# Later maxima for batch 1, another order of weight tiles, and casts on VectorE in an attention + FFN kernel

## The chip, the core and the metric

One NeuronCore of a Trainium2 chip runs the whole program. The metric is the device time of one execution in microseconds; the median of 3 runs before is 716.87 us (716.13 to 718.10). In this text PE is TensorE, DVE is VectorE, ACT is ScalarE, SP is the engine whose queue issues the loads and stores.

## The reference

Linear-memory attention in 8 batches of 8 heads, 576 tokens, head size 64, 32 memory slots, and a SiLU feed-forward layer over all tokens:

```python
a = exp(phi - max(phi, axis=2)); a = a / (sum(a, axis=2) + 1e-9)      # [8, 8, 576, 32]
k_m = einsum('bhsm,bhsd->bhmd', a, k); v_m = einsum('bhsm,bhsd->bhmd', a, v)
scores = q @ k_m.T / sqrt(64)
attn = softmax(scores); x = (attn @ v_m) as [4608, 512]
h = x @ w_in            # w_in [512, 2048]
g = h * sigmoid(h)
out = g @ w_out         # w_out [2048, 512], all float32
```

## The kernel before, in words

Inputs are float32 in a layout made beforehand; the two weights come as 64-bit words, which the kernel itself turns into float32. To keep float32 accuracy, every large product is done as three products of a high part and a low part: `wo_hi`/`wo_lo` for w_out, `ghi`/`glo` (both in the tile `gparts`) for the activations, `ahi`/`alo` (`aparts`) for the attention and two halves of `pparts` for the product of v_m and w_in, which replaces x @ w_in: first p = v_m @ w_in per head, then h = attn @ p.

**The main loop.** For each batch b there are 16 steps, one for each 128 columns of d_ff. Step fc does `ffn1` on PE (12 matmuls into the one PSUM tile `h`), `silu` on ACT (`g`, 512 tokens, and `gleft`, 64 tokens; `h` is free when gleft is done), `split` (ghi is a cast of g, glo is g minus ghi), and then, in two halves of two token tiles each, `ffn2` of the step before: per token tile three matmuls, ghi by wo_hi, ghi by wo_lo, glo by wo_hi, into `acc`. After every second batch four `left` steps do the remaining tokens.

**Slots.** All other work hangs on a table `events`: `ev(b, slot, fn)` puts fn behind a half step; slot 5 is behind the first half of step 5's ffn2, slot 5.5 behind its second half. In batch 0 these are the p tiles (`p_mm`, 256 columns each, at 2.5, 4.5, 6.5 ...), the conversions of the weights (`conv_next`) and the attention of batch 1, whose slots stand in `at_slot`: mx (maxima of phi, `phi_max` on DVE), sub (the maxima brought together by transposes on PE, `phi_allmax`, and half a step later back to all partitions, and `phi_sub`), ex (`phi_exp` on ACT), em (`e_mm`: 80 matmuls into `bg`, then `kvn`, k_m and v_m normalised, one half by ACT, one by DVE), tr (`e_tr`: kvn transposed on PE, copied to `kvT`), s0 and s1 (scores), and the softmax. `bg` is one PSUM tile: p tiles, maxima, e, transposes and scores all use it in turn, and each waits until the one before has been read out (for a p tile by `p_split`: hi on ACT, lo on DVE, line 575).

**Weights.** Both are cut in 8 tiles of 256 columns or rows, here called i0 to i7 (w_in) and o0 to o7 (w_out). `w_load` brings a tile into `raw`, of which there are 3 buffers; a tile of w_in comes in two halves. Two early tiles, o1 and i2, have a home inside `win` instead. `w_conv` turns a tile into float32: two ACT instructions (lines 166 and 168), a shift and an add on DVE (lines 170 and 172), and for w_out two more, wo_hi on ACT (174) and wo_lo on DVE (176). Then its raw buffer is free. `conv_next` converts the next tile of the list `to_conv` and then asks for the next of `to_load`. Tile i(j) is needed by the p tile at slot 2j-1.5, tile o(j) by ffn2 in step 2j+1.

**What sets the order.** PE and SP keep the order in which the program is written; in batch 0 the order of DVE and ACT is chosen by the framework's scheduler when the program is built and then is fixed. Each engine takes its instructions in that order and waits at the head. So a load that waits for a raw buffer holds up every load behind it on SP.

Of the kernel before, what the change touches and what calls it, by code (L numbers as in the profile page):

```python
# [24 lines left out]
DMODEL, DFF = 512, 2048  # L25
NFC = DFF // P
CW = 256
# [21 lines left out]
def attn_ffn_kernel(  # L49
# [9 lines left out]
    nc = tc.nc  # L59
# [115 lines left out]
            elif kind == "o":  # L175
                nc.vector.tensor_tensor(wo_lo[:, fc], to, wo_hi[:, fc], op=ALU.subtract)  # L176

    to_load = iter([(k, j) for j in range(1, DFF // CW) for k in "io"])
    to_conv = iter([(k, j) for j in range(1, DFF // CW) for k in "io"])

    def load_next(few=False):
        w = next(to_load, None)
# [396 lines left out]
    def ffn1(b, fc):  # L579
        hi, lo = pj[b, fc * P // JW]  # L580
        fs = slice(fc * P % JW, fc * P % JW + P)
        ahi, alo = at[b]["ahi"], at[b]["alo"]
        h = ps.tile([P, 2, 512], F32, tag="h", name="h", bufs=1)
        for hf in range(2):
            sl = slice(hf * HALF, (hf + 1) * HALF)
            n = 0
            for wt, a in ((hi, ahi), (hi, alo), (lo, ahi)):
                for p in range(2):
                    nc.tensor.matmul(h[:, hf, :HALF], wt[:, p, fs], a[:, p, sl], start=n == 0, stop=n == 5)  # L589
                    n += 1  # L590
        return h

    turn = iter(range(1 << 30))

    def split(g32, on_act=False, steps=(0, 1), gs=None):
        if gs is None:
            n = next(turn) % 2
            gs = gparts[:, 0, n], gparts[:, 1, n]
        ghi, glo = gs
        if 0 in steps:  # L600
            if on_act:
                nc.scalar.copy(ghi, g32)  # L602
            else:
                nc.vector.tensor_copy(ghi, g32)  # L604
        if 1 in steps:
            nc.vector.tensor_tensor(glo, g32, ghi, op=ALU.subtract)  # L606
        return gs

    def silu(b, fc, h):
        g32 = sb.tile([P, MAIN], F32, tag="g32", name="g32", bufs=2)  # L610
        w = MAIN // 2
        nc.scalar.activation(g32.rearrange("p (h f) -> p h f", h=2), h[:, :, :w], AF.Silu)  # L612
        o = b % 2 * LEFT
        nc.scalar.activation(  # L614
            gleft[:, fc, o : o + LEFT].rearrange("p (h f) -> p h f", h=2), h[:, :, w:HALF], AF.Silu
        )
        return g32
# [36 lines left out]
    def ev(b, slot, fn, *a):  # L654
        events.setdefault((b, slot), []).append((fn, a))

    for b in range(B):
        if b == 0:
            for j in range(2, DFF // CW):
                ev(b, 2 * j - 1.5, p_mm, b, j * CW, CW)  # L660
        else:
            for j in range(1, NJ):
                ev(b, 4 * j - 3, p_mm, b, j * JW, JW)
        n = b + 1
        if n == B:
            continue
        at_slot = (2, 3, 4, 5.5, 7.5, 9.5, 11.5, 11.5, 12, 12.5, 12.5, 13) if b == 0 else (0, 1, 2, 3, 4, 6, 7, 8, 9, 10, 11, 12)
        mx, sub, ex, em, tr, s0, s1, sx, se, ss, sn, sk = at_slot
        ev(b, mx, phi_max, n)
        if n == 1:  # L670
            ev(b, sub, phi_allmax, n, (0, 1), (0,))
            ev(b, sub + 0.5, phi_allmax, n, (0, 1), (1,))
        else:
            for i in range(3):
                ev(b, sub, phi_fold, n, i)
        ev(b, sub + 0.5, phi_sub, n)
        ev(b, ex, phi_exp, n)
        ev(b, em, e_mm, n)
        if n + 1 < B:
            ev(b, 14 if b == 0 else em + 1, load_kv, n + 1)  # L680
        ev(b, tr, e_tr, n)
        ev(b, s0, s_mm, n, 0)
        ev(b, em, load_q, n, 1)
        ev(b, s1, s_mm, n, 1)
        if n + 1 < B:
            ev(b, s1, load_q, n + 1, 0)
        ev(b, sx, s_max, n, ALL)
        ev(b, sx, s_sub, n, ALL)
        ev(b, se, s_exp, n, ALL)
        ev(b, ss, s_sum, n, ALL)  # L690
        ev(b, sn, s_norm, n, ALL)
        ev(b, sk, s_back, n, ALL)
        ev(b, sk, s_low, n, ALL)
        if n + 1 < B:
            ev(b, sk, load_phi, n + 1)
        ev(b, 14, p_mm, n, 0, JW)
    for k in range(1, DFF // CW * 2 - 2):
        ev(0, max(1.5, k - 1), conv_next)

# [8 lines left out]
    with in_order(DVE, ACT) as last:  # L710
# [62 lines left out]
        w_conv(O0, 0, "hal")  # L773
        w_conv(I1, None, "p")
        gs = split(silu(0, 0, ffn1(0, 0)))
        w_conv(I1, None, "csa")
        w_conv(O0, 1, "sh")
        g32 = silu(0, 1, ffn1(0, 1))
        g1 = split(g32, steps=(0,))
        main_step(0, 0, gs, (0, 1))  # L780
        p_mm(0, CW, CW)
        main_step(0, 0, gs, (2, 3))
        split(g32, steps=(1,), gs=g1)
        w_conv(O0, 1, "al")
        prev = ("main", 0, 1, g1)
# [8 lines left out]
    def finish(tiles):  # L794
        if prev is None:
            return
        if prev[0] == "main":
            main_step(prev[1], prev[2], prev[3], tiles)
        elif tiles[0] == 0:
            left_step(prev[1], prev[2], prev[3])  # L800

    for b in range(B):
        if b == 1:
            whole.close()
        for fc in range(NFC):
            if b == 0 and fc < 2:
                for part in range(2):
                    for fn, a in events.pop((b, fc + part / 2), []):
                        fn(*a)
                continue  # L810
            h = ffn1(b, fc)
            gs = split(silu(b, fc, h), b == 0 and fc < 7)
            for part in range(2):
                finish((2 * part, 2 * part + 1))
                for fn, a in events.pop((b, fc + part / 2), []):
                    fn(*a)
            prev = ("main", b, fc, gs)
        if b % 2:
            for n in range(NLS):
                gs = split(gleft[:, n * NI : (n + 1) * NI].rearrange("p c f -> p (c f)"))  # L820
                finish((0, 1, 2, 3))
                prev = ("left", b, n, gs)
# [3 lines left out]
def build(arrays, bacc, num_devices=1):  # L826
    nc = bacc.Bacc("TRN2", target_bir_lowering=False, num_devices=1, dynamic_dma_scratch_size=1024)
    aps = [
        nc.dram_tensor(n, a.shape, mybir.dt.from_np(a.dtype), kind="ExternalInput").ap() for n, a in arrays.items()
    ]  # L830
    out = nc.dram_tensor("out", (B * S, DMODEL), F32, kind="ExternalOutput").ap()
    with tile.TileContext(nc) as tc:
        attn_ffn_kernel(tc, *aps, out)
    return nc
# [44 lines left out]
```

## Time and profile before

| what | before |
|---|---|
| median of 3 runs | 716.87 us |
| the profiled execution | 715.9 us, its span 714.1 us |
| PE busy | 696.7 us, 98% of the span |
| DVE busy, ACT busy | 364.6 us (51%), 260.7 us (37%) |
| granted PE clock | 0.999 |

The span runs from the first to the last instruction of the program. Rows of the order of time read: start, length, engine, line, operation, tiles, and in brackets the idle time of the engine just before and the instruction that ended it. Rows of a group read: busy us, mean ns of one, then idle us before them. Busy PE is not PE at its peak. Line numbers are those of the kernel before; in the changed one they differ by one or two.

### The profile page before, as it was taken

To read this page: it belongs to the slowest core of one execution; us is meant where nothing else is said; L and a number is where in the kernel's file an instruction comes from. 1 tells how busy PE (TensorE), PEld (TensorE's weight loads), DVE (VectorE), ACT (ScalarE), POOL (GpSimd) and SP (SyncE) were. 2 spreads that over 40 slices of the span, in tenths; PEclk is the share of its full clock that TensorE was granted. 3 is DMA by queue.
4 is the path that set the end of the run, shared out by engine and by line. 5 is a ranking of instruction groups with operands and counts; after the bars stand their busy time and mean duration, and the time that the engine had idled before them with its cause. 6 is when DMAs were issued, how large, how long until landed. Compare 5 with 4: busy or idle time off the path is not lost.

```text
span 714.1 us, 11570 instructions
## 1 busy us (share of the span) xinstructions
PE 696.7 (98%) x4833; PEld 556.4 (78%) x4833; DVE 364.6 (51%) x653; ACT 260.7 (37%) x459; POOL 0.7 (0%) x6
## 2 busy tenths in 40 slices
PE   7879999999999999999999999999999999999997
PEld 3567677878888788877888778787888878888885
DVE  3897877356353563637346373635636355233322
ACT  2799744324223242524124241332322324132211
POOL 0000000000000000000000000000000000000000
PEclk9999999999999999999999999999999999999999
DMA  9967605321023210132010320131101000010002
GB/s 344 388 232 241 238 34 226 134 68 34 1 74 133 68 34 1 60 139 74 23 60 15 135 71 30 61 134 67 34 9 65 2 1 1 0 60 1 1 1 74
DMA packets 25444, 60.14 MB, mean 84 GB/s; under 512 B 2096, under 2 KB 10416, under 8 KB 25392
## 3 DMA queue, kind: packets, MB, share of 16 engines
q1 hardware_dynamic: 24672, 57.02, 22.8%
q10 hardware_dynamic: 720, 2.38, 0.9%
q8 instruction: 38, 0.62, 0.4%
q14 instruction: 14, 0.11, 0.1%
HBM read 49.95 MB, written 9.44 MB: 83 GB/s over the span
## 4 chain that ended last, share of the span: by engine, by line
PE 82%; DVE 5%; ACT 5%; issue 1%; DMA 1%; DVEq 0%; ACTq 0%; SPq 0%
PE acc L626 44%; PE h L589 25%; PE accleft L626 6%; PE bg L559 4%; PE bg L309 2%; PE bg L353 1%; DMA raw<-in_w_in 1%; DVE gparts L606 1%; ACT L612 1%; ACT g L612 1%; ACT phi L297 1%; DVE wo_lo L176 1%; ACT pparts L573 1%; DVE phi L289 1%; ACT raw L168 1%
## 5 line engine op out<-in xcount | busy, mean ns | idle before, releaser
L626 PE MATMUL acc<-wo_hi,gparts 128*128 128x512 f32 x1024 | 352.1, 397 | 0.5 <-DVE gparts L606 0.5
L626 PEld LDWEIGHTS acc<-wo_hi,gparts 128*128 128x128 f32 x1024 | 192.0, 188 | 66.8 <-issue 29.8
L589 PEld LDWEIGHTS h<-aparts,pparts 128*128 128x128 f32 x1536 | 215.2, 188 | 17.9 <-ACT gleft L614 5.6
L589 PE MATMUL h<-aparts,pparts 128*128 128x288 f32 x1536 | 225.9, 296 | 1.8 <-ACT gleft L614 1.1
L626 PE MATMUL acc<-wo_lo,gparts 128*128 128x512 f32 x512 | 201.2, 393 | 0.4 <-DVE wo_lo L176 0.4
L612 ACT ACTIVATE g<-h 128x512 f32<-128x512 f32 x128 | 76.4, 597 | 305.4 <-issue 179.6
L604 DVE CAST gparts<-g 128x512 fp32r<-128x512 f32 x123 | 52.3, 425 | 220.7 <-ACT g L612 219.9
L626 PEld LDWEIGHTS acc<-wo_lo,gparts 128*128 128x128 f32 x512 | 96.1, 188 | 15.2 <-DVE wo_lo L176 0.7
L606 DVE TENSOR_TENSOR gparts<-g,gparts 128x512 fp32r<-128x512 f32 x128 | 88.1, 688 | 11.9 <-ACT gparts L602 1.3
L575 DVE TENSOR_TENSOR pparts<-bg,pparts 128x1024 fp32r<-128x1024 f32 (+1 forms) x36 | 39.5, 1098 | 37.4 <-ACT pparts L573 37.4
L573 ACT ACTIVATE pparts<-bg 128x1024 fp32r<-128x1024 f32 (+1 forms) x36 | 33.3, 926 | 28.8 <-PE bg L559 28.8
L626 PE MATMUL accleft<-wo_hi,gparts 128*128 128x512 f32 x128 | 40.6, 389 | 0.0
L559 PE MATMUL bg<-win,kvT 64*32 64x512 f32 (+1 forms) x576 | 35.8, 554 | 0.9 <-DVE win L172 0.8
L614 ACT ACTIVATE gleft<-h 128x64 f32<-128x64 f32 x128 | 28.0, 219 | 0.0
L626 PEld LDWEIGHTS accleft<-wo_hi,gparts 128*128 128x128 f32 x128 | 24.0, 188 | 4.9
L632 ACT ACTIVATE o<-acc 128x512 f32<-128x512 f32 x32 | 19.1, 598 | 21.3 <-PE acc L626 10.7
L626 PE MATMUL accleft<-wo_lo,gparts 128*128 128x512 f32 x64 | 24.9, 389 | 0.0
L612 ACT ACT_TABLE_LOAD x14 | 18.0, 1283 | 8.0 <-PE h L589 7.9
L559 PEld LDWEIGHTS bg<-win,kvT 64*32 64x32 f32 x576 | 6.6, 104 | 14.3 <-issue 12.9
L604 DVE CAST gparts<-gleft 128x512 fp32r<-128x512 f32 x16 | 6.8, 427 | 20.7 <-PE accleft L626 12.2
L168 ACT ACTIVATE raw<-raw 128x1024 int32<-128x1024 uint32 (+1 forms) x16 | 16.5, 1030 | 0.0
L391 DVE TENSOR_REDUCE ssm<-sc 128x36 f32<-128x1152 f32 x7 | 9.5, 1353 | 8.8 <-ACT sc L387 8.8
(123 smaller groups left out, 369.3 us busy)
## 6 DMA issues: line engine op xcount, KB each, us to landing
kv<-in_kv SPq DMA_DIRECT2D x28, 516.0 KB, 6.2
q<-in_q SPq DMA_DIRECT2D x16, 576.0 KB, 3.8
out<-o SPq DMA_DIRECT2D x32, 256.0 KB, 2.1
raw<-in_w_in SPq DMA_DIRECT2D x14, 512.0 KB, 6.6
raw<-in_w_out SPq DMA_DIRECT2D x6, 1024.0 KB, 6.4
phi<-in_phi SPq DMA_DIRECT2D x7, 576.0 KB, 3.8
kv<-in_kv ACTq DMA_DIRECT2D x4, 516.0 KB, 6.2
kr<-in_kv SPq DMA_DIRECT2D x7, 258.0 KB, 7.4
```

What stands on the lines that cost most here:

```text
L168: nc.scalar.activation(r, low, AF.Copy, scale=2.0**-29)
L309: nc.tensor.matmul(pt[p][M * r : M * (r + 1), :KVW], e[:, p, c, M * r : M * (r + 1)], kvt[c][:, p, r], start=c == 0, stop=False, skip_grou ...
L559: nc.tensor.matmul(bg[M * r : M * (r + 1), p, :w].rearrange("p (k f) -> p k f", f=P), kvT[D * p : D * (p + 1), 1, r], win[D * p : D * (p + ...
L573: nc.scalar.activation(hi[:, :, c], bg[:, :, :w], AF.Copy)
L575: nc.vector.tensor_tensor(lo[:, :, c], bg[:, :, :w], hi[:, :, c], op=ALU.subtract)
L589: nc.tensor.matmul(h[:, hf, :HALF], wt[:, p, fs], a[:, p, sl], start=n == 0, stop=n == 5)
L604: nc.vector.tensor_copy(ghi, g32)
L606: nc.vector.tensor_tensor(glo, g32, ghi, op=ALU.subtract)
L612: nc.scalar.activation(g32.rearrange("p (h f) -> p h f", h=2), h[:, :, :w], AF.Silu)
L614: nc.scalar.activation(gleft[:, fc, o : o + LEFT].rearrange("p (h f) -> p h f", h=2), h[:, :, w:HALF], AF.Silu)
L626: nc.tensor.matmul(acc[key], gt[:, cs], wt[:, fc], start=fc == 0 and n == 0, stop=fc == NFC - 1 and n == 2)
L632: nc.scalar.activation(o, acc.pop(key), AF.Copy)
```

## The change

Three edits.

1. The first four attention slots of batch 1 in batch 0 move: mx 2 to 4, sub 3 to 5, ex 4 to 6, em 5.5 to 7.5; tr moves from 7.5 to 8. The slots from s0 on stay.
2. Tiles are asked for and converted in another order: i(j+1) ahead of o(j). Conversions were i2 after o1, then o2, i3, o3, i4 ... at slots 2, 3, 4, 5 ...; now i2 comes ahead of o1, and then i3 at 3, o2 at 3.5, i4 at 5, o3 at 5.5, i5 at 7, o4 at 7.5, up to o7 at 12.5.
3. ghi of steps 2 to 6 of batch 0 was cast by ACT; now DVE casts all.

```diff
-    to_load = iter([(k, j) for j in range(1, DFF // CW) for k in "io"])
-    to_conv = iter([(k, j) for j in range(1, DFF // CW) for k in "io"])
+    later = [w for j in range(2, DFF // CW) for w in (("i", j + 1), ("o", j))][:-2] + [("o", DFF // CW - 1)]
+    to_load = iter([("i", 1), ("o", 1), ("i", 2)] + later)
+    to_conv = iter([("i", 1), ("i", 2), ("o", 1)] + later)
...
-    def split(g32, on_act=False, steps=(0, 1), gs=None):
+    def split(g32, steps=(0, 1), gs=None):
...
-            if on_act:
-                nc.scalar.copy(ghi, g32)
-            else:
-                nc.vector.tensor_copy(ghi, g32)
+            nc.vector.tensor_copy(ghi, g32)
...
-        at_slot = (2, 3, 4, 5.5, 7.5, 9.5, 11.5, 11.5, 12, 12.5, 12.5, 13) if b == 0 else (0, 1, 2, 3, 4, 6, 7, 8, 9, 10, 11, 12)
+        at_slot = (4, 5, 6, 7.5, 8, 9.5, 11.5, 11.5, 12, 12.5, 12.5, 13) if b == 0 else (0, 1, 2, 3, 4, 6, 7, 8, 9, 10, 11, 12)
...
-    for k in range(1, DFF // CW * 2 - 2):
-        ev(0, max(1.5, k - 1), conv_next)
+    for slot in [1.5, 1.5] + [2 * j - 1 if k == "i" else min(2 * j - 0.5, 12.5) for k, i in later for j in [i - 1 if k == "i" else i]]:
+        ev(0, slot, conv_next)
...
-            gs = split(silu(b, fc, h), b == 0 and fc < 7)
+            gs = split(silu(b, fc, h))
```

How the order of the engines moves, at three places. First SP, the loads behind the first half of batch 1's q (in a row of `in_w_in` two halves of one tile). Before: o2, i3, o3, i4, o4, i5.

```order
L87 DMA q1_0_428<-in_q 128x1152
L87 DMA raw_430<-in_w_out 128x2x512
L87 DMA raw_432<-in_w_in 128x4x128 x2
L87 DMA raw_435<-in_w_out 128x2x512
L87 DMA raw_444<-in_w_in 128x4x128 x2
L87 DMA raw_451<-in_w_out 128x2x512
L87 DMA raw_490<-in_w_in 128x4x128 x2
```

Now: i3, o2, i4, o3, i5, o4, i6.

```order
L87 DMA q1_0_428<-in_q 128x1152
L87 DMA raw_430<-in_w_in 128x4x128 x2
L87 DMA raw_433<-in_w_out 128x2x512
L87 DMA raw_435<-in_w_in 128x4x128 x2
L87 DMA raw_442<-in_w_out 128x2x512
L87 DMA raw_451<-in_w_in 128x4x128 x2
L87 DMA raw_523<-in_w_out 128x2x512
L87 DMA raw_538<-in_w_in 128x4x128 x2
```

With three buffers taken in turn, i5 now takes the buffer of o2; before, the tile in the fourth place, i4, took it.

Second DVE, from the conversion of i2 and o1 to the maxima of batch 1 (`mt`, `mx`); g_466 here is g of step 2, g_523 of step 3. Before, with no cast, since ACT did it:

```order
L172 ISA win<-win,cva 128x1024x2
L172 ISA win<-win 128x2048
L176 TENSOR_TENSOR wo_lo<-win,wo_hi 128x1024
L606 TENSOR_TENSOR gparts<-g_466,gparts 128x512
L238 TENSOR_TENSOR mt<-phi_416 128x512
L170 TENSOR_SCALAR cva<-cva 128x1024
L239 TENSOR_TENSOR mx<-mt 128x256
L172 ISA raw<-raw,cva 128x1024x2
L241 TENSOR_TENSOR mx<-mx,phi_416 64x128 x2
L176 TENSOR_TENSOR wo_lo<-raw,wo_hi 128x1024
L575 TENSOR_TENSOR pparts<-bg,pparts 128x2x256
L606 TENSOR_TENSOR gparts<-g_523,gparts 128x512
```

Now the same stretch holds no maxima; g_467 is g of step 2, g_508 of step 3.

```order
L172 ISA win<-win 128x2048
L172 ISA win<-win,cva 128x1024x2
L602 CAST gparts<-g_467 128x512
L176 TENSOR_TENSOR wo_lo<-win,wo_hi 128x1024
L604 TENSOR_TENSOR gparts<-g_467,gparts 128x512
L576 TENSOR_TENSOR pparts<-bg,pparts 128x2x256
L602 CAST gparts<-g_508 128x512
L170 TENSOR_SCALAR win<-win 128x1024
L604 TENSOR_TENSOR gparts<-g_508,gparts 128x512
L172 ISA win<-raw,win 128x2048
L170 TENSOR_SCALAR cva<-cva 128x1024
L172 ISA raw<-raw,cva 128x1024x2
```

i2's add (`win<-win`) now stands ahead of o1's, pparts ahead of o2, and the maxima follow behind o2's add.

Third ACT, ahead of its half of kvn (g_621 is g of step 5, g_699 of step 7, g_795 of step 8). Before, kvn stood between steps 5 and 6:

```order
L612 ACTIVATE g_621<-h 128x512
L614 ACTIVATE gleft<-h 128x64
L602 CAST gparts<-g_621 128x512
L166 ACTIVATE cva<-raw 128x1024
L168 ACTIVATE raw<-raw 128x1024
L174 ACTIVATE wo_hi<-cva 128x1024
L166 ACTIVATE win<-raw 128x1024
L168 ACTIVATE raw<-raw 128x1024
L331 ACTIVATE kvn<-bg,rs 128x2x64
```

Now, between steps 7 and 8:

```order
L610 ACTIVATE g_699<-h 128x512
L612 ACTIVATE gleft<-h 128x64
L168 ACTIVATE raw<-raw 128x1024
L174 ACTIVATE wo_hi<-cva 128x1024
L166 ACTIVATE win<-raw 128x1024
L168 ACTIVATE raw<-raw 128x1024
L166 ACTIVATE cva<-raw 128x1024
L168 ACTIVATE raw<-raw 128x1024
L332 ACTIVATE kvn<-bg,rs 128x2x64
L610 ACTIVATE g_795<-h 128x512
```

Five conversion instructions stood between g and kvn before, six now, of the tiles o4, i6 and o5, and the cast is gone.

## The prediction

> **What bounds the kernel now.** I read the page first, then who waited for whom on PE, then PE's order of time between 36 and 112 us, then the same stretch on DVE, ACT and the load queue, with groups of lines for the prices.
>
> ```profile
> span 714.1 us, 11570 instructions
> ...
> PE 696.7 (98%) x4833; PEld 556.4 (78%) x4833; DVE 364.6 (51%) x653; ACT 260.7 (37%) x459; POOL 0.7 (0%) x6
> ```
>
> PE sets the end: only its idle time can be won or lost. Between step 2 of batch 0 and the scores of batch 1 it stands five times, 0.36+0.78+2.85+0.48+1.15 = 5.62 us together; that is all the change can reach. In order of time (start, length, engine, line, operation; idle time before and what ended it in brackets):
>
> ```profile
> 39.07 0.50 PE L626 MATMUL acc<-wo_lo,gparts 128*128 128x512 f32 x1 [0.36 <-DVE wo_lo L176]
> ...
> 42.64 0.67 PE L559 MATMUL bg<-win,kvT 64*32 64x256 f32 x16 [0.78 <-DVE win L172]
> 43.23 1.86 PE L589 MATMUL h<-aparts,pparts 128*128 128x288 f32 x12
> ...
> 49.33 0.44 PE L250 MATMUL bg<-ident,mx 128*128 128x128 f32 x2 [2.85 <-DVE pparts L575]
> ...
> 51.36 1.83 PE L589 MATMUL h<-aparts,pparts 128*128 128x288 f32 x12
> ...
> 56.46 1.85 PE L589 MATMUL h<-aparts,pparts 128*128 128x288 f32 x12
> ...
> 63.27 1.86 PE L589 MATMUL h<-aparts,pparts 128*128 128x288 f32 x12
> ...
> 72.99 0.38 PE L339 MATMUL bg<-ident,kvn 128*128 128x128 f32 x2
> ...
> 81.34 0.73 PE L626 MATMUL acc<-wo_hi,gparts 128*128 128x512 f32 x2 [0.48 <-DVE gparts L606]
> ...
> 85.06 0.72 PE L353 MATMUL bg<-q,kvT 64*32 64x288 f32 x16 [1.15 <-DVE pparts L575]
> ...
> 101.25 1.85 PE L589 MATMUL h<-aparts,pparts 128*128 128x288 f32 x12
> ...
> 105.69 1.75 PE L589 MATMUL h<-aparts,pparts 128*128 128x288 f32 x12
> ```
>
> Step lengths follow: a bare step 105.69-101.25 = 4.44; with a p tile 56.46-51.36 = 5.10; with e's 80 matmuls 63.27-56.46 = 6.81. Why PE waits there is on DVE and ACT, nearly full from 36 to 92 us:
>
> ```profile
> 36.00:92.00 56.00, 50.20 (x412) 38.98 (x411) 48.64 (x71) 49.56 (x67) 0.00 (x0) 1.00 0.65 224
> ```
>
> (Columns: PE, PEld, DVE 48.64 of 56, ACT 49.56 of 56.) The grant stays at 1.00, so the clock takes no part.
>
> **The 2.85 us** is DVE's backlog: the maxima, o1's and o2's conversions and the release of bg by `p_split` queue up:
>
> ```profile
> 39.54 0.69 DVE L170 TENSOR_SCALAR win<-win 128x1024 uint32<-128x1024 uint32 x1
> ...
> 41.27 1.22 DVE L172 CUSTOM_DVE_ANT_0 win<-win 128x2048 uint16<-128x2048 uint16 x1
> 42.41 1.23 DVE L176 TENSOR_TENSOR wo_lo<-win,wo_hi 128x1024 fp32r<-128x1024 f32 x1
> ...
> 44.16 0.67 DVE L238 TENSOR_TENSOR mt<-phi 128x512 f32<-128x512 f32 x1
> ...
> 45.71 1.21 DVE L172 CUSTOM_DVE_ANT_0 raw<-raw,cva 128x2048 uint16<-128x2048 uint16 x1
> ...
> 47.45 1.23 DVE L176 TENSOR_TENSOR wo_lo<-raw,wo_hi 128x1024 fp32r<-128x1024 f32 x1
> 48.59 0.68 DVE L575 TENSOR_TENSOR pparts<-bg,pparts 128x512 fp32r<-128x512 f32 x1
> ```
>
> Back to back, a row of 1.22 starts the next 1.14 later (47.45 to 48.59), one of 0.69 0.60 later. With that I walk the new DVE order. From 38.9: two shifts 1.20, two adds 2.28, the cast of step 2 0.34, wo_lo of o1 1.14, glo 0.61, pparts 0.60: 45.1. The cast of step 3 waits for ACT's g until 45.2, then cast 0.34, shift 0.60, glo 0.61, i3's add 1.14, shift 0.60, o2's add 1.14, i4's shift 0.60, mt 0.60, wo_lo of o2 1.22: it ends at **52.2**. Then cast, mx, glo, two small mx and pparts, which ends about 54.5 and frees bg. The maxima's transposes stand ahead of step 5's third tile, where PE comes at 52.1+1.7+1.4 = 55.2 (below): 2.85 goes to 0. Their second half, behind DVE's cm, is ready at 56.5 and wanted at 56.8; I leave 0.1 for both.
>
> **The 0.78 us** goes: i2's adds now stand ahead of o1's, one 1.22 us row earlier, where 0.78 was missing. The price is o1: ghi's cast and glo of step 2 now have `wo_lo` of o1 between them (cast at 42.4, wo_lo at 42.8, glo 43.9 to 44.6), and PE wants glo at about 44.4: 0.3 lost.
>
> **The 1.15 us** belongs to i7, which was late:
>
> ```profile
> 73.76 0.93 SPq L87 DMA_DIRECT2D raw<-in_w_in  x2
> ...
> 82.55 1.13 ACT L166 ACTIVATE win<-raw 128x1024 f32<-128x1024 f32 x1 [3.13 <-DMA raw<-in_w_in]
> ```
>
> ACT stood 3.13 us before it with the eviction of bg behind it. In the new order i7 is asked for when o4's buffer is free, about 71, so it lands about 76 and this wait goes. The 0.48 (glo behind o6's adds) goes too; the 0.36 lies ahead of the change and stays.
>
> **The casts.** Five go from ACT to DVE:
>
> ```profile
> L602 ACT CAST gparts<-g 128x512 fp32r<-128x512 f32 x5 | 3.1, 619 | 0.0
> ...
> L604 DVE CAST gparts<-g 128x512 fp32r<-128x512 f32 x5 | 2.1, 418 | 1.2 <-ACT g L612 1.2
> ...
> L606 DVE TENSOR_TENSOR gparts<-g,gparts 128x512 fp32r<-128x512 f32 x10 | 6.8, 683 | 1.4 <-ACT gparts L602 1.3
> ```
>
> ACT gains 3.1 - 5x0.1 of overlap = 2.6 us, DVE loses 5x0.34 = 1.7. DVE has 7.4 us idle in the stretch, ACT 6.4, so neither sum decides; bounds are a gain of 1.3 (the wait L606 had for ACT) and a loss of 1.7 if every cast lay on the path. I take 0: both are already inside the walk along the new order that gives the other terms.
>
> **What costs nothing.** The exp moves with its two table loads, as many as before, and they are in ACT's sum below. q's second half moves with e's slot behind o6 on the load queue, asked for at about 73; even at i7's 8.3 it lands by 82, and the second scores of step 11 want it about 91. Without that cover it would cost what i7 cost, 1.15.
>
> **What is late next: e.** The order before gave e's matmuls and the transposes of kvn two steps: 72.99-63.27 = 9.7 us on PE. Now they are half a step apart: ffn1 and two tiles, 1.7+1.4 = 3.1 us. When does PE arrive, when is kvn ready?
>
> PE: step 3 starts at 42.2; + 4.44+0.3 = 47.0 (step 4); + 5.10 = 52.1; + 4.44 and 0.55 for the maxima's small matmuls = 57.1; + 5.10 = 62.2; + 6.81 = 69.0 (step 8); + 3.1 = 72.1.
>
> kvn: it hangs on i5. i5's buffer is o2's and comes free when DVE has written wo_lo of o2, at 52.2 by the walk above. What a tile of w_in takes from there, and what ACT's rows cost:
>
> ```profile
> 57.26 0.92 SPq L87 DMA_DIRECT2D raw<-in_w_in  x2
> ...
> DMA to landing us min/median/max: 3.7/4.2/4.8
> ...
> L168 ACT ACTIVATE raw<-raw 128x1024 int32<-128x1024 uint32 x11 | 12.6, 1144 | 0.0
> L174 ACT ACTIVATE wo_hi<-cva 128x1024 fp32r<-128x1024 f32 x7 | 7.4, 1059 | 0.3 <-DVE cva L170 0.3
> L166 ACT ACTIVATE cva<-raw 128x1024 f32<-128x1024 f32 x6 | 7.1, 1177 | 0.7 <-DVE kvT L342 0.7
> L166 ACT ACTIVATE win<-raw 128x1024 f32<-128x1024 f32 x5 | 5.8, 1153 | 3.1 <-DMA raw<-in_w_in 3.1
> ...
> L612 ACT ACT_TABLE_LOAD x1 | 1.3, 1283 | 0.0
> ...
> 56.88 1.17 ACT L297 ACTIVATE phi<-phi 128x1152 f32<-128x1152 f32 x1
> ...
> 67.16 0.36 ACT L331 ACTIVATE kvn<-bg,rs 128x128 f32<-128x128 f32 x1
> ...
> 75.19 0.28 DVE L342 COPY kvT<-bg 128x128 f32<-128x128 f32 x1
> ...
> 76.61 0.24 ACT L343 COPY kvT<-bg 128x128 f32<-128x128 f32 x1
> ```
>
> The two halves issue at 52.2 and 52.6; the second takes 4.8: i5 lands at 57.4. ACT idles before it (gleft of step 5 is done at 55.8), and from 57.4 to kvn never stops. By the new order, with 0.1 of overlap each: win 1.05, wo_hi 0.95, raw 1.03, g and gleft 0.61, table 1.28, exp 1.06, pparts 0.49, cva 1.06, table 1.28, g and gleft 0.61, raw 1.03, wo_hi 0.95, win 1.05, raw 1.03, cva 1.06, raw 1.03, kvn 0.37: 15.9, so 73.3. DVE's half of kvn writes the same tile, waits for ACT's, 0.35 and two hand-overs more: 73.8. PE stands from 72.1 to 73.8: **1.7 to 1.9 us**, I take 1.8. Behind it the p tile of step 8 waits for bg, which ACT's copy of kvT frees: DVE copies at 75.6 behind a 1.22 us add and a cast, ACT's 0.24 ends 75.9, PE is there at 73.8+0.3+1.4 = 75.5: **0.4 us**.
>
> Sum: -2.85+0.1 -0.78+0.3 -1.15 -0.48 +1.8+0.4 = **-2.6 us**. The span goes from 714.1 to 711.5, the execution from 715.9 to 713.3, and the median of 716.87 (three runs, 716.13 to 718.10), 1.0 above that execution, to **714.3**. In bounds: e's wait 0 to 5, so a gain of 4.8 to a loss of 0.6.
>
> The Trainium skill ("DMA: Bandwidth & Descriptors", section "Anatomy of one DMA — SWDGE (gpsimd) path") fits transfers issued by software with about 2.0 us fixed and bytes over 436 GB/s; as an estimate from that page i5's 1 MB would land 4.4 us after its first issue, at 56.6, and the gain would be 3.4, inside the forecast's own range. The quoted rows, 0.41 us to the second issue and 4.8 from there, say 5.2, and the rows decide.
>
> **The rivals.**
>
> *Late loads, 0.22.* i7's halves took 7.2 and 8.3 us, where the tile quoted above took 3.7 and 4.8:
>
> ```profile
> DMA to landing us min/median/max: 7.2/7.8/8.3
> ```
>
> It had o6 and q in flight before it. In the new order i5 stands with no slack: each us it is late is a us of PE. At i7's price, 8.3 instead of 4.8, +3.5: -2.6+3.5 = +0.9, 717.8; at half of it 716.0. Against it: i5 follows its o by 4 us, alone, and q now stands behind o6. I price the case at 716.5, within the bound. The Trainium skill (same page, "Why a DMA increments its semaphore by 16 and not by 1") says that engines of one transfer finish independently and only all 16 mean landed; this one late tile fits, and does not prove it.
>
> *Slower, 0.07.* The three raw buffers form a ring: a late tile delays its conversion, that the next issue, that ACT again. If i5 and i6 both take 8.3, i5 costs 3.5; i6 is asked for at 62.2 (o3's wo_lo), lands at 67.4 and ACT comes to it at 57.4+11.4 = 68.8, so 1.4 of its 3.5 is covered: 3.5+2.1-2.6 = +3.0, 719.9. It is slower by 0.3% once the two cost PE more than 2.6+2.15 = 4.8 us. For: i6 is asked for with o5 1.5 us behind it. Against: it needs two late tiles where one was seen.
>
> *The maxima's wait stays, 0.09.* DVE carries 1.7 us of casts more ahead of them; if these land whole at the maxima, the gain is 0.9: 716.0.
>
> *e does not wait, 0.10.* If ACT gets ahead, by an i5 landing 2 us early or a PE that is slower by as much, the 2.2 go: gain 4.8, 712.1.
>
> **How the numbers follow.** Forecast 0.52; own range 713.4 to 715.2, from e's wait at 1 to 2.7. A measurement of this kernel tells no change from about 0.3%, 2.15 us: faster is under 714.7. The forecast's range lies to some 85% under it: 0.44, with the last rival 0.54. Same: 0.08+0.22+0.09 less a little, 0.38. Slower 0.08. The range 712.4 to 717.6 leaves out the ring and the tails.
>
> **What would show it.** Right: PE waits under 0.5 us at the maxima's transposes, none at the scores, 1 to 2.7 at the transposes of kvn, released by DVE's kvn, with ACT back to back from i5's landing near 57.4; step 13 starts near 98.6 instead of 101.25. Wrong: ACT waiting for a w_in or w_out tile elsewhere, PE waits for h or glo above 0.5, or a wait of over 1 us left at the maxima.

## The result, and the profile after

| | before | after |
|---|---|---|
| first series, median | 716.44 us (8 executions, 715.68 to 718.10) | 712.58 us (8, 711.31 to 714.51) |
| ratio, 95% interval | | 0.9948 (0.9933 to 0.9963) |
| second series, beside other kernels | 716.04 us | 714.45 us (11, 712.69 to 715.30) |
| ratio, 95% interval | | 0.9976 (0.9961 to 0.9990) |
| profiled execution, span | 715.9, 714.1 us | 714.5, 712.7 us; in the second series 713.0, 711.3 us |

Faster in both series, by 0.5 and by 0.2%; the forecast was 714.3 us, 0.36% under before. The first profile was taken of the slowest of the eight executions of its series, the second of one of the faster ones. The start of an execution differs by up to 2 us from one profile to the next, so all traces are compared below by one **distance**: from the first product of step 0 to the first product of step 14, both on PE. In before it is 105.69 - 28.17 = 77.5 us:

```profile
28.17 0.53 PE L589 MATMUL h<-aparts,pparts 128*128 128x288 f32 x2
```

The page of the changed kernel, first profile:

```profile
span 712.7 us, 11569 instructions
...
PE 697.3 (98%) x4833; PEld 556.6 (78%) x4833; DVE 366.4 (51%) x658; ACT 258.7 (36%) x454; POOL 0.7 (0%) x6
```

Five instructions have gone from ACT to DVE, the casts. PE is as busy as before; what counts is again where it is not. PE in order of time, at the places that the prediction quoted of before:

```profile
27.89 0.53 PE L590 MATMUL h<-aparts,pparts 128*128 128x288 f32 x2
...
38.81 0.50 PE L624 MATMUL acc<-wo_lo,gparts 128*128 128x512 f32 x1 [0.37 <-DVE wo_lo L176]
...
41.55 0.66 PE L560 MATMUL bg<-win,kvT 64*32 64x256 f32 x16
...
54.85 0.38 PE L251 MATMUL bg<-ident,mx 128*128 128x128 f32 x2
...
75.59 0.44 PE L340 MATMUL bg<-ident,kvn 128*128 128x128 f32 x2 [3.16 <-DVE kvn L334]
...
79.47 1.86 PE L590 MATMUL h<-aparts,pparts 128*128 128x288 f32 x12
...
84.02 0.72 PE L354 MATMUL bg<-q,kvT 64*32 64x288 f32 x16
...
104.52 1.75 PE L590 MATMUL h<-aparts,pparts 128*128 128x288 f32 x12
```

No bracket is left at i2's p tile (0.78 before), at the maxima (2.85) and at the scores (1.15). In their place stands one wait of 3.16 us at the transposes of kvn. The distance is 76.6 us, only 0.9 less than before. Behind the wait something else happens. In the same profile, by microseconds (columns: busy time of PE, PEld, DVE, ACT and POOL, then the granted clock):

```profile
76.00:77.00 1.00, 1.00 (x4) 0.75 (x3) 1.00 (x3) 0.70 (x1) 0.00 (x0) 0.50 0.89 307
77.00:78.00 1.00, 1.00 (x4) 0.66 (x2) 1.00 (x3) 0.77 (x2) 0.00 (x0) 0.50 0.97 381
78.00:79.00 1.00, 1.00 (x18) 0.23 (x16) 1.00 (x2) 1.00 (x2) 0.00 (x0) 0.50 1.05 430
79.00:80.00 1.00, 1.00 (x20) 0.53 (x5) 0.84 (x2) 1.00 (x2) 0.00 (x0) 0.80 0.78 321
```

PE is fully busy at half its clock for some 3.4 us. ACT in the same profile says what kvn waited for:

```profile
57.48 1.16 ACT L166 ACTIVATE win<-raw 128x1024 f32<-128x1024 f32 x1 [1.72 <-DMA raw<-in_w_in]
...
72.76 1.12 ACT L166 ACTIVATE cva<-raw 128x1024 f32<-128x1024 f32 x1 [1.33 <-DMA raw<-in_w_out]
...
74.79 0.36 ACT L332 ACTIVATE kvn<-bg,rs 128x128 f32<-128x128 f32 x1
```

i5 comes at 57.48, ACT then works without a gap to 71.4, and stands 1.33 us for o5, which is queued ahead of kvn: issued at 63.8, it needs 8.8 us. Of the three transfers asked for between 62 and 66 us, the two halves of i6 and o5:

```profile
DMA to landing us min/median/max: 3.6/4.7/8.8
```

### The profile page after: what moved, and what is told of

Same layout as the page of the kernel before. It is cut to its first block, busy times and chain, and to the rows that moved or that the text cites. A ratio compares the mean times of both kernels' runs of the same rounds, so it can differ in the third digit from the quotient of the medians.

```text
span 712.7 us, 11569 instructions
## 1 busy us (share of the span) xinstructions
PE 697.3 (98%) x4833; PEld 556.6 (78%) x4833; DVE 366.4 (51%) x658; ACT 258.7 (36%) x454; POOL 0.7 (0%) x6
## 4 chain that ended last, share of the span: by engine, by line
PE 84%; DVE 5%; ACT 2%; DMA 1%; issue 1%; ACTq 0%; SPq 0%
PE acc L624 45%; PE h L590 25%; PE accleft L624 6%; PE bg L560 4%; PE bg L310 2%; PE bg L354 1%; DMA raw<-in_w_out 1%; DVE phi L290 1%; DVE gparts L604 1%; ACT L610 1%; ACT phi L298 0%; ACT pparts L574 0%; DVE raw L172 0%; PE bg L318 0%; DVE win L172 0%
## 5 line engine op out<-in xcount | busy, mean ns | idle before, releaser
L602 DVE CAST gparts<-g 128x512 fp32r<-128x512 f32 x128 | 54.4, 425 | 223.2 <-ACT g L610 222.6
```

## The experiments

Distances and ratios to before (medians of before in the four series: 716.34, 716.04, 716.50 and 716.42 us):

| kernel | distance, us | median, us | ratio (95%) |
|---|---|---|---|
| slots alone | 77.6 | 716.13 | 0.9998 (0.9989 to 1.0006) |
| order alone, twice | 74.1, 74.3 | 712.23, 713.02 | 0.9953 (0.9938 to 0.9967), 0.9951 (0.9936 to 0.9967) |
| casts alone | 74.4 | 713.12 | 0.9960 (0.9948 to 0.9972) |
| order and casts | 75.1 | 713.97 | 0.9971 (0.9960 to 0.9982) |
| slots and order | 79.4 | 717.65 | 1.0016 (0.9997 to 1.0035) |
| slots and casts | 76.7 | 715.14 | 0.9996 (0.9984 to 1.0007) |
| all three: the change, twice | 76.6, 73.9 | 712.58, 714.45 | 0.9948 (0.9933 to 0.9963), 0.9976 (0.9961 to 0.9990) |
| the change and zero products | 74.1 | 713.94 | 0.9966 (0.9950 to 0.9981) |
| the change, e earlier | 73.5 | 714.24 | 0.9965 (0.9949 to 0.9980) |
| the change, kvn first | 74.4 | 711.82 | 0.9937 (0.9923 to 0.9951) |
| that, small work ahead of late tiles | 72.2 | 710.94 | 0.9921 (0.9903 to 0.9938) |

### The three edits one by one

**Slots alone.**

```diff
-        at_slot = (2, 3, 4, 5.5, 7.5, 9.5, ...
+        at_slot = (4, 5, 6, 7.5, 8, 9.5, ...
```

> Before, with the new slots alone; the order of the tiles and ACT's early ghi casts stay as before. Theory A (the order of the tiles carries the gain, because it lets ACT's conversions and with them the phi steps come earlier): the maxima's wait of 2.85 us does not go, since the matching DVE operations still stand behind the same conversions; some 1.6 us of it are left at the maxima, the wait of 1.0 for i2 stays, and e's later slot brings a new wait of about 1.7 at the transposes of kvn and 0.8 at the p tile behind it. About 717.6 us, 1.2 above before. Theory B (the two later slots carry the gain, as a reader of the change in words would think): the maxima's wait is gone with nothing in its place, about 713.6 us.

Measured 716.13 us, no change. Who waited for whom on PE, between 34 and 100 us of this kernel (total, times, longest):

```profile
PE bg L250 <- DVE pparts L575: 1.6, 1, 1.6
PE bg L339 <- DVE kvn L333: 1.6, 1, 1.6
PE bg L256 <- DVE cm L251: 1.1, 1, 1.1
PE bg L559 <- DVE win L172: 0.8, 1, 0.8
PE bg L559 <- ACT kvT L343: 0.6, 1, 0.6
```

Theory B falls: the later slot does not rid the maxima of their wait. Every wait that theory A listed is there, and one of 1.1 at cm. Its time was 1.5 too high: the waits of 1.15 and 0.48 that stood in before around i7's late conversion are not there, though no tile was moved.

Where the difference comes from is seen on the load queue. q's second half hangs on the slot of em, so the slots move it too: in before it is asked for at 69.53, ahead of i7 (73.76), here at 78.29, behind i7 (75.78). i7's two halves, which took 7.2 and 8.3 us in before, take here:

```profile
DMA to landing us min/median/max: 3.6/4.1/4.7
```

All 14 profiles part in this way: with the old slots (five profiles) i7's second half lands 7.5 to 8.3 us after its issue, with the new ones (nine) 4.7 to 5.1. No run moved q alone, so that q is the cause is likely, but not shown.

**Order alone.**

```diff
-    to_load = iter([(k, j) for j in range(1, DFF // CW) for k in "io"])
-    to_conv = iter([(k, j) for j in range(1, DFF // CW) for k in "io"])
+    later = [w for j in range(2, DFF // CW) for w in (("i", j + 1), ("o", j))][:-2] + [("o", DFF // CW - 1)]
+    to_load = iter([("i", 1), ("o", 1), ("i", 2)] + later)
+    to_conv = iter([("i", 1), ("i", 2), ("o", 1)] + later)
...
-        ev(0, max(1.5, k - 1), conv_next)
+        ev(0, slot, conv_next)
```

> Before, with the new order of loads and conversions alone; slots and ACT's casts stay. Theory A: the waits for i2 (0.78) and for the late tiles behind i7 (1.15) and 0.48 are gone, the maxima's wait shrinks from 2.85 to about 1.3, e does not wait: about 713.0 us. Theory B (the slots carry the gain): only the waits for i2 and i7 go, the maxima's 2.85 stays: about 714.5 us.

> The new order of loads and conversions alone a second time, beside the others' runs: by its own first runs a ratio of 0.9953 (0.9938 to 0.9967), with waits of 1.0 at the maxima and 0.7 at the scores, none over 2 us and so no half clock in the middle. If the slots and the casts are worth anything on top of it, the changed kernel's ratios (0.9948 and 0.9976) lie under this one's; if they are worth nothing, this stays at 0.995.

712.23 and 713.02 us: theory A, twice. The waits on PE in the first of the two:

```profile
PE bg L251 <- DVE mx L242: 1.0, 1, 1.0
PE bg L354 <- DVE pparts L576: 0.7, 1, 0.7
PE acc L627 <- DVE wo_lo L176: 0.4, 1, 0.4
PE h L590 <- ACT gleft L615: 0.3, 1, 0.3
```

i2's wait is gone, the maxima's has shrunk from 2.85 to 1.0 in their old slots. i7 is late here too (7.5 us; ACT stands 1.84 us before it), but less waits behind it: 0.7 is left at the scores. This one edit has the whole gain of the change: its two ratios lie between the change's two, so nothing can be told of what the other two edits add to it.

**Casts alone.**

```diff
-            gs = split(silu(b, fc, h), b == 0 and fc < 7)
+            gs = split(silu(b, fc, h))
```

> Before, with ghi cast by DVE in fc steps 0 to 6 of batch 0 as everywhere else; slots and order stay. Forecast of the prediction's term (casts cost nothing, bounds -1.3 to +1.7): about 716.4. Worked out from the rows: ACT is freed of seven casts, so its conversions end sooner and the maxima's wait falls by some 0.6 to about 2.3, the other waits stay: about 715.8. Rival (a DVE cast of every half tile delays the conversions' subtractions on DVE, and with them the tiles): up to 718.1.

713.12 us: 3 us faster, where 0 was forecast and 0.6 worked out from the rows. All three numbers on record missed. i2's 0.8 and 2.0 at the maxima stay, about as worked out; what had not been seen is at the scores. ACT of this kernel:

```profile
79.41 0.58 ACT L573 ACTIVATE pparts<-bg 128x512 fp32r<-128x512 f32 x1
...
81.78 1.19 ACT L166 ACTIVATE win<-raw 128x1024 f32<-128x1024 f32 x1 [0.24 <-DMA raw<-in_w_in]
```

i7 lands as late as in before (issued at 73.74, here 8.0 us, there 8.8). But the scheduler, with five casts gone from ACT, has put the eviction of bg ahead of i7's conversion, while in before it stood behind it:

```profile
83.57 0.60 ACT L573 ACTIVATE pparts<-bg 128x512 fp32r<-128x512 f32 x1
```

So the scores do not wait. Of the 3.1 us that the distance falls, 2.1 are in step 9, where before has this wait of 1.15 and glo's 0.48, and 0.6 are in step 3, at the maxima. So most of the gain comes with the new place of a few instructions, and not from ACT's 2.6 us spread over the steps. (The casts are five, not the seven of the expectation.)

**Order and casts, without the slots.**

> The changed kernel with the slots of before: order of tiles and casts alone. Theory A: the maxima's wait is down to some 1.3, those for i2, i7 and the 0.48 gone, e does not wait, and no stretch at half clock follows: about 713.2 us, the same as the changed kernel within 0.7. Theory B (the slots carry the gain): about 714.5 or more. A third theory, that the half clock after e's wait in the changed kernel costs it as much as its slots gain: this one is as fast as the changed kernel or faster, 711.5 to 712.6.

713.97 us, between A and B. The third theory missed its time of 711.5 to 712.6, and this kernel, with no half clock in these steps, is not faster than the change; its ratio lies between the change's two, so "as fast" is not excluded. It is 1.3 us slower than order alone by their ratios (same series), which is at the edge of what the intervals tell, and 1.0 by the distances: four short waits, 1.0 at the maxima, 0.7 at the transposes of kvn, 0.6 for glo and 0.4 for gleft, where order alone has three.

**Slots and order, slots and casts.**

> The changed kernel with ACT's early ghi casts of before: slots and order without the DVE casts. Theory A (the casts cost on top of the order, as the runs so far have it: order alone 712.2, order and casts 714.0): about 711 to 711.5. Theory B (each part moves the list-scheduled order on ACT and DVE in its own way, and the parts do not add; by the orders that result, ACT is busier by seven casts ahead of kvn, so e's wait at the transposes of kvn is longer, some 2.4 with every tile in time, and a new wait of 1.1 stands at the transposes of cm): 713.5 to 715.

> Before, with the new slots and the DVE casts, in the old order of tiles. Theory A (the parts add: slots nothing, casts -3.2): 713.1. Theory B (they do not add; by the resulting orders the wait for i2 of 0.8 to 1.0 stays, the maxima still wait 1.6, cm 0.9, kvn 1.5 and the p tile behind it 0.8): 716 to 718, no gain over before.

Both times theory B: the parts do not add. Slots and casts: 715.14, 0.9 under the range that B gave, but no gain that can be told (ratio 0.9996), with the five waits of the list at 0.8, 1.5, 0.6, 1.5 and 0.3. Slots and order: 717.65 us, above the range that B gave. ACT is later there by its casts, a late o4 holds it up (2.44 us), and e's wait is longer than anywhere:

```profile
78.55 0.47 PE L340 MATMUL bg<-ident,kvn 128*128 128x128 f32 x2 [4.44 <-DVE kvn L334]
```

The granted clock behind it, in the same kernel:

```profile
79.00:80.00 1.00, 1.00 (x4) 0.81 (x3) 1.00 (x3) 1.00 (x2) 0.00 (x0) 0.50 1.03 381
80.00:81.00 1.00, 1.00 (x4) 0.68 (x3) 0.88 (x2) 0.51 (x2) 0.00 (x0) 0.50 0.99 402
81.00:82.00 1.00, 1.00 (x18) 0.23 (x16) 0.70 (x1) 0.48 (x1) 0.00 (x0) 0.50 0.94 349
```

So the casts are worth -2.9 us alone, +1.3 on top of the order (at the edge of the noise), and -3.2 on top of order and slots (717.65 to 714.45, same series). The slots are worth nothing alone, +4.5 on top of the order (by the ratios of two series), and on top of order and casts -1.6 by the one series and +0.4 by the other.

### Late o5 and the half clock

**The change once more.**

> The changed kernel itself once more, for a second profile beside the others' runs. Theory A (how late tile o5 of w_out lands differs from one execution to the next, e's wait follows it, and the half clock comes only when that wait passes about 3 us): another wait at the transposes of kvn than 3.16, and if it is under 2.85, the granted clock stays 1.00 behind it and step 14 starts 73.5 to 75.0 us after step 0 instead of 76.6. Theory B (o5 always lands 8.8 us after its issue, the wait and the half clock stand in every execution, and the runs differ only at the start): the wait is 3.1 to 3.3 again, with a stretch at 0.50, and the same 76.6. Median 712.6 by both, ratio 0.993 to 0.9965.

The second profile, PE:

```profile
29.07 0.53 PE L590 MATMUL h<-aparts,pparts 128*128 128x288 f32 x2
...
75.43 0.44 PE L340 MATMUL bg<-ident,kvn 128*128 128x128 f32 x2 [1.92 <-DVE kvn L334]
...
77.99 1.86 PE L590 MATMUL h<-aparts,pparts 128*128 128x288 f32 x12
...
98.57 1.85 PE L590 MATMUL h<-aparts,pparts 128*128 128x288 f32 x12
...
103.01 1.75 PE L590 MATMUL h<-aparts,pparts 128*128 128x288 f32 x12
```

Theory A as to the profile: o5 took 7.5 us here, ACT did not wait for it, e's wait is 1.92, the clock stays at 1.00 and the distance is 73.9. The 2.7 us between two profiles of one program are 1.24 of wait (3.16 - 1.92) and 1.3 of clock: from the transposes to the next step 3.88 us (75.59 to 79.47) against 2.56. The median did not hold, 714.45 for 712.6. Of the 11 executions the three with a mean clock of 0.998 or more took 712.7 to 713.0 us, the other eight 713.1 to 715.3; in the first series five of 8 were at 0.998 or more. The mean does not tell where the clock was lost: the second profile of order alone, a kernel with no wait above 1.0 in these steps, has a stretch at 0.66 while the program starts, and so have those of slots alone and of order and casts.

```profile
20.00:25.00 5.00, 4.35 (x28) 1.93 (x29) 3.59 (x7) 3.70 (x9) 0.00 (x0) 0.66 1.06 379
```

**Products with zeros in e's wait.** `add_zeros` issues matmuls of 128x512 with the zeros as weights into `acc[0, 1]`. DVE's and ACT's orders are held by explicit dependencies, as the build of the changed kernel has them.

```diff
+    zeros = const.tile([P, P], mybir.dt.bfloat16, name="zeros")
+    nc.gpsimd.memset(zeros, 0.0)
...
+        if n == 1:
+            ev(b, tr, add_zeros, 8)
```

> The changed kernel, with the order of DVE's and ACT's instructions held as it is, and eight bf16 matmuls of zero weights added to an output's accumulator (they add zero) just ahead of the transposes of kvn, so that PE works for some 2.2 us of e's wait. Clock theory: the granted clock stays 1.00 behind the transposes whatever e's wait, the matmuls run inside the wait, and the median is 0 to 0.9 us under the changed kernel's (it gains 1.7 in those executions in which the wait passed 3 us). Rival (the half clock has nothing to do with the wait): the stretch at 0.50 stays where o5 is late, and the median is the changed kernel's or up to 0.4 above it.

713.94 us, ratio 0.9966 against 0.9976, intervals overlapping: not told apart. The profile has the eight matmuls in 1.90 us and a rest of the wait:

```profile
72.65 1.90 PE L656 MATMUL acc<-ident,zeros 128*128 128x512 bf16 x8
74.80 0.44 PE L344 MATMUL bg<-ident,kvn 128*128 128x128 f32 x2 [0.24 <-DVE kvn L338]
```

Without them PE would have stood some 2.1 us, and waits of up to 2.85 us at such places left the clock at 1.00, so this profile is no test. The executions are a hint: a mean clock under 0.998 in 3 of 11, against 8 of 11 of the change on the same chip. That is for the clock theory, and too few to show it; and the eight with the better clock took 712.5 to 715.7 us, so their clock alone does not make them faster than the change.

**e half a slot earlier.**

```diff
-        at_slot = (4, 5, 6, 7.5, 8, 9.5, ...
+        at_slot = (4, 5, 6, 7, 8, 9.5, ...
```

> The changed kernel with the matmuls of e at 7 in the place of 7.5. Theory A (e's chain reaches ACT and DVE before o5's conversions and kvn is placed ahead of them): no wait at the transposes of kvn, but the copies of kvT now come behind the conversions, so that the p tile after them waits some 2.0; no half clock, since 2.0 is under 2.85; step 14 starts about 73.7 us after step 0, and the ratio is 0.9945 to 0.996. Theory B (kvn's place on ACT is not changed by half a slot): the wait stays at the transposes, 1.9 to 3.2, and the ratio is the changed kernel's.

Theory A in every place: no wait at kvn, and the next one behind the copy of kvT.

```profile
PE bg L560 <- ACT kvT L344: 1.7, 1, 1.7
PE acc L624 <- DVE wo_lo L176: 0.4, 1, 0.4
```

The distance is 73.5, the time 714.24 us (0.9965): just above the expected ratio of 0.9945 to 0.996, and not to be told from the change.

**kvn first.** What this kernel's build moves on ACT (DVE alike: reciprocals and kvn ahead of i6's add and o5's shift):

```diff
-L167 ACTIVATE cva<-raw 128x1024
-L169 ACTIVATE raw<-raw 128x1024
-L333 ACTIVATE kvn<-bg,rs 128x2x64
+L333 ACTIVATE kvn<-bg,rs 128x2x64
+L167 ACTIVATE cva<-raw 128x1024
+L169 ACTIVATE raw<-raw 128x1024
+L345 COPY kvT_807<-bg 128x128
 L611 ACTIVATE g_795<-h 128x512
 L613 ACTIVATE gleft<-h 128x64
 L175 ACTIVATE wo_hi<-cva 128x1024
-L345 COPY kvT_807<-bg 128x128
```

> The changed kernel with the orders of DVE's and ACT's instructions fixed by explicit dependencies, and in them one piece moved: kvn (with the reciprocals ahead of it) stands before the two conversions of o5 on ACT and before the shift and merge of i6 and o5 on DVE, and the copies of kvT follow sooner. Theory A (e's wait is made by what is queued ahead of kvn on ACT, o5's conversions and the wait for o5's landing): PE's wait at the transposes of kvn falls from 1.9 to 3.2 to about 0.3 whatever o5 does, no half clock follows it, 0.3 appears at the p tile and up to 0.9 at the scores; step 14 starts about 73 to 73.5 us after step 0, and the ratio to before is about 0.993 to 0.9955, at or under the changed kernel's. Theory B (the wait is e's own chain, from the matmuls of e over the sums and reciprocals): 1.5 or more stays at the transposes, and the time is the changed kernel's.

Theory A. e's wait was made by the queue ahead of kvn, not by e:

```profile
PE h L591 <- ACT gleft L613: 1.2, 1, 1.2
PE bg L355 <- DVE pparts L577: 1.0, 1, 1.0
PE acc L625 <- DVE wo_lo L177: 0.4, 1, 0.4
PE bg L341 <- DVE kvn L335: 0.2, 1, 0.2
```

0.2 is left, though o5 again took 8.0 us. The 1.0 at the scores was expected, the 1.2 for gleft not, so the distance is 74.4 for 73 to 73.5. 711.82 us, ratio 0.9937. All six executions had a mean clock of 0.999 or 1.000.

**Small work ahead of late tiles.** On top of it, the evictions and silus that stood behind conversions of late tiles go ahead of them, on ACT:

```diff
+L575 ACTIVATE pparts<-bg 128x2x256
 L167 ACTIVATE win<-raw 128x1024
 L169 ACTIVATE raw<-raw 128x1024
-L575 ACTIVATE pparts<-bg 128x2x256
...
-L167 ACTIVATE cva<-raw 128x1024
 L611 ACTIVATE g_895<-h 128x512
 L613 ACTIVATE gleft<-h 128x64
-L169 ACTIVATE raw<-raw 128x1024
-L175 ACTIVATE wo_hi<-cva 128x1024
 L575 ACTIVATE pparts<-bg 128x2x256
+L167 ACTIVATE cva<-raw 128x1024
+L169 ACTIVATE raw<-raw 128x1024
 L611 ACTIVATE g_936<-h 128x512
 L613 ACTIVATE gleft<-h 128x64
+L175 ACTIVATE wo_hi<-cva 128x1024
```

> The kernel with kvn first, and in the same fixed orders the small work of steps 8 to 10 moved ahead of the conversions of late tiles: on ACT the p tile's eviction before the conversion of i7, and silu of step 9 with the next p tile's eviction before that of o7, on DVE what belongs to them. Theory A (PE's waits of 0.95 at the scores and 1.21 at step 11 in the run before come of ACT standing at a tile that has not landed, with evictions queued behind it): both are gone, step 14 starts 72.3 to 72.7 us after step 0, and the time is some 2 us under that of the kernel with kvn first: a ratio to before of 0.990 to 0.9925. Theory B (the waits come of the late tiles' own data, which PE needs there): the waits stay, as does the ratio, 0.993 to 0.995.

Theory A: all that PE waits for between 34 and 100 us in this kernel is

```profile
PE acc L625 <- DVE wo_lo L177: 0.4, 1, 0.4
PE bg L341 <- DVE kvn L335: 0.3, 1, 0.3
```

The distance is 72.2 us, 5.3 less than before, and the time 710.94 us, ratio 0.9921 (0.9903 to 0.9938): the fastest of all, 5.5 us under before. It was not run beside the changed kernel; its interval lies under that of the change's second series and meets the first's by 0.0005. It also overlaps that of kvn first (0.9923 to 0.9951), so that this last step gained anything rests on the distance, 74.4 to 72.2.

## Why the prediction was right, point by point

Its sum was -2.6 us; the two series give -3.9 and -1.6. The second median lies in its own range of 713.4 to 715.2 us, the first, 712.58, below it and within the wider one. It was right mostly for the reason it gave: the waits that it named went, and e's came in their place. But it had errors on both sides that offset each other, and one term went for a reason that it named only in passing. Of the marks that it gave for being wrong, ACT standing at tiles elsewhere is seen in both profiles (3.0 and 2.7 us at tiles of w_out between 34 and 100 us), though PE pays for it only in the first, at o5; there e's wait of 3.16 is also above the 1 to 2.7 that it allowed. Since the profiles start at different times, places are given below in us after step 0.

- **The maxima's 2.85, i2's 0.78, i7's 1.15 and the 0.48** went, all to nothing (no bracket at any of the four rows). The walk put the maxima's transposes at 27.0 (55.2 - 28.17), and 27.0 (54.85 - 27.89) is where they are. What the walk could not say is by which edit: slots alone leave 1.6, order alone 1.0, and only the two together bring it to 0 (in slots and order 1.0 stays at their second half, behind cm, which is gone with the casts).
- **Why i7's 1.15 went** is half right. The tile was asked for at 43.1 and landed at 48.6 us (42.8 and 47.8 forecast). But order alone asks for it earlier, at 41.4 us, and gets it nearly as late as before, its second half 7.5 us behind its issue (8.3 in before): its lateness goes in all profiles with the slots, which put q behind it, and not with the earlier request. The prediction knew that q was ahead of i7 in before and behind o6 now; it didn't make this the reason.
- **0.3 for glo of step 2 and 0.4 at the p tile behind kvn** were priced and cost nothing: no wait is listed at either in the two profiles. They are the mis-sized terms on the pessimistic side.
- **i5's landing and ACT back to back to kvn**: forecast at 29.2 and 45.1 us; ACT starts on i5 at 29.6 and 29.5, and on kvn at 46.9 (45.6 without the 1.33 for o5) and 45.6. kvn is half a microsecond later than the walk had it, and so is PE, which comes to the transposes at 44.5 and 44.4, where 43.9 was forecast. That the two errors cancel is luck.
- **e's wait of 1.8** is at the place, of the cause and, where o5 lands before ACT comes to it, of the size predicted: 1.92 in the second profile, 3.16 - 1.33 = 1.83 in the first. Step 13 was to start 70.4 us after step 0; it does at 69.5 in the second profile and at 72.2 in the first, where before has 73.1.
- **The late-load rival** was priced for i5. The tile that made PE wait longer is o5, which the walk took to be in time. It adds 1.2 between the two profiles, within the bound that was kept for a late tile.
- **"The clock takes no part"** is the step that failed in the first profile. It read the granted 1.00 of before, where the longest wait is 2.85 us, and carried it to a kernel whose new wait could be 5 by its own bounds. In the first profile it costs 1.3 us. Without late o5 and half clock the change would have been worth some 3.6 us (distance 77.5 to 73.9), 1.0 more than the sum.
- **Casts at 0** was right only as part of the walk over the whole new order. As a term it has no single value: -2.9, +1.3 or -3.2 us by what stands beside it. The bounds given, -1.3 to +1.7, did not hold two of these three, because they counted the casts' own time and not what the scheduler does with the place they leave, as the moved eviction in casts alone shows.

What stays open: why the change's two series differ. The share of executions with a lower mean clock differs with them (3 of 8, 8 of 11), but the profiles show two places where the clock falls, the start and e's wait, and the executions without a profile do not say which it was.

## What to carry to other kernels

On an engine that takes its work in order, an instruction that waits for a transfer holds up whatever is queued behind it; small evictions that the busiest engine waits for go ahead of conversions whose tile may be late. Here it took the distance from 76.6 or 73.9 us down to 72.2, which no slot did. Where a scheduler chooses the order, an edit's price is not the time of the instructions that it moves: read the new order around every wait, on the load queue too, where the slots moved q, and try the parts alone before one is credited with the gain.

## What the hardware did that was not expected

PE's granted clock fell to 0.50 for some 3.4 us behind e's wait where this was 3.16 and 4.44 us long, and not behind waits of 1.92, 2.0 or 2.85 us in steps 3 to 8; both times the stretch behind it took 3.88 us, where it takes 2.56 at full clock. So each of the two cost PE 1.3 us on top of the wait. But the length of one wait does not settle it. While the program starts, the clock fell in the same way, for some 3.4 us, in three of the 14 profiles, after waits of 1.80 us (order alone, second profile), 1.81 us (order and casts) and only 0.86 us (slots alone). In slots alone (columns: busy time of PE, clock, DMA share, GB/s):

```profile
20.00:25.00 5.00, 5.00 (x32) 0.66 1.06 380
```

Before has the same waits there, 0.74 and 0.86 us, and its clock stays at 1.00. What else decides is open. The Trainium skill ("TensorE: Matmul & The Clock Gate", section "Why this matters for your kernels") asks for no idle gap above about 3 us between bursts of matmuls; in steps 2 to 14 the traces agree, but at the start the clock fell without such a gap. In its section "What's actually happening" the clock is halved after one idle window of about 3.4 us; a wait of 3.16 us was enough here, and at the start shorter ones, and the measurement decides.

The same tile o5, asked for 1.5 us behind i6, took 8.8, 7.5 and 8.0 us in three profiles with the same order of loads up to it (the change twice, kvn first), and 7.5 or 7.6 in the other three of that order, so a wait for it is not one number but a range.
